# Normalization moved ahead, inner sums on POOL, chunk loads on SyncE and respread sums in a fused attention and feed-forward kernel

## The chip, the cores and the metric

The kernel runs on one core of one Trainium2 chip. The metric is the device time of one execution in microseconds, the median of several runs. The engines of the core are TensorE (PE in the profile, its weight loads PEld), VectorE (DVE), ScalarE (ACT), GpSimd (POOL) and SyncE (SP), which here only issues transfers. Each engine runs its own instructions in order, and semaphores tie the engines together.

## What is computed

An attention with a hash mask, whose output becomes the tokens of a feed-forward layer with a sigmoid-approximated gelu:

```python
# q, k, v: (4, 8, 768, 64); proj: (64, 6); w_in: (512, 2048); w_out: (2048, 512)
q_bucket = np.sum((np.einsum('bhsd,dk->bhsk', q, proj) > 0) * 2 ** np.arange(6), axis=-1)
k_bucket = np.sum((np.einsum('bhsd,dk->bhsk', k, proj) > 0) * 2 ** np.arange(6), axis=-1)
mask = q_bucket[:, :, :, None] == k_bucket[:, :, None, :]
scores = np.where(mask, np.matmul(q, k.transpose(0, 1, 3, 2)) / np.sqrt(64), -1e9)
attn = np.exp(scores - np.max(scores, axis=-1, keepdims=True))
attn = attn / (np.sum(attn, axis=-1, keepdims=True) + 1e-09)
x = np.matmul(attn, v).transpose(0, 2, 1, 3).reshape(3072, 512)
h = x @ w_in
out = (h * (1.0 / (1.0 + np.exp(-1.702 * h)))) @ w_out
```

The weights arrive as 64-bit floats, and the kernel turns them into 32-bit ones itself.

## The kernel before

The program has three stages, and TensorE, VectorE, ScalarE and POOL run exactly in the order in which the program is written (`manual_schedule` for these four). SyncE's queue is not among them: the framework's planner orders the transfers on it by the times at which it expects them to be ready.

**Attention** (to about 316 us) works on 16 pairs of heads. `invert` and `norm` divide a pair's result by its sums, on VectorE; for the last pair they are written at the end of `attention`, after `next(ff)`, which emits the first step of the feed-forward layer. Meanwhile VectorE converts chunks of w_in (`convert`, six steps on VectorE and a square on ScalarE for each chunk of 512 columns, with a single buffer `raw` for the load). Two late chunks of w_in and the 16 chunks of w_out are converted during the next stage (`conversions`), and their loads are issued by ScalarE (`queue=nc.scalar`), each right after the fourth step of the chunk before has freed `raw`.

**The first product, x @ w_in** (about 316 to 612 us), is Strassen's scheme in Winograd's form with seven products instead of eight. The operands' sums are made ahead: `in_sums` (POOL, lines 211 to 214) for the weights, two column blocks a call, and `x_sums` (VectorE, lines 219 to 222, by `sums_b`) for the tokens; `x_sums` has four parts, of which the first gives t1, the second changes b12 in place, the third gives t2 and the fourth t4. Product 5 uses t1, product 7 the changed b12, product 6 uses t2 and product 4 uses t4. There are three groups of 1024 tokens and eight column blocks in each, 24 steps. Steps 0, 1 and 20 to 23 are written by `hidden`, a step each; steps 2 to 19 are nine pairs t = 1 to 9, written by `pair_of_steps`. In a pair, products 2 and 3 of both steps are themselves split once more (`nested`) into seven small products of 256 columns; the operands' inner sums are `nest_w` (POOL) for the weights and `nest_x` (lines 797 to 800, VectorE) for the activations, once for each group of tokens. After each small product VectorE adds it to a result (line 750), and the next small product that shares its PSUM bank waits for that addition. `u`, `v`, `c22` and `c21` are a step's results, copied or activated by ScalarE; `g_outer` forms four outer sums `t`, `v` from them on POOL, and `keep` stores each to `g_dram` by SyncE.

A pair has ten numbered places (`hook(1)` to `hook(10)`) at which other work is written between the products: steps of a conversion, `in_sums` for later blocks, `nest_w`, and, at a change of tokens (the end of t = 3 and 7, then t = 4 and 8), `x_sums` and `nest_x` for the next group. The order around the front half of a pair is `p1(0)`, hook 1, `p1(1)`, hook 2, `p6(0)`, hook 3, `p6(1)`, hook 4, `p5(0)`, hook 5, `p7(0)`; `old()` between them writes the small products that the pair before has left over, one at a time. Product 6 of the first step is `p6(0)`.

**The second product** (about 612 us to the end) runs seven of these outer products for each of three groups, 21 steps of seven products (`product_of_halves`, line 1080). `g_sums` (VectorE) forms the operands' sums one step ahead, `inner_sums` (POOL) those of w_out; in steps 5 and 6 a tiny copy into `mark` holds POOL until a result of the step before is there. In the last but one step, `after` writes the third part of `g_sums`, t2, twice.

Of the kernel before, what the change touches and what calls it, by code (L numbers as in the profile page):

```python
# [8 lines left out]
F32 = mybir.dt.float32  # L9
# [4 lines left out]
Alu = mybir.AluOpType  # L14
# [5 lines left out]
P = 128  # L20
# [18 lines left out]
def kernel(  # L39
# [17 lines left out]
    nc = tc.nc  # L57
# [82 lines left out]
    t_x = const.tile([P, 3, KC // 2, 512], F32, name="t_x")  # L140
# [67 lines left out]
    def sums_a(eng, a11, a12, s3, a22, s1, s2, s4, a21=None):  # L208

        a21 = s3 if a21 is None else a21  # L210
        return [lambda: eng.tensor_tensor(s1, a21, a22, op=Alu.add),
                lambda: eng.tensor_tensor(s3, a11, a21, op=Alu.subtract),
                lambda: eng.tensor_tensor(s2, s1, a11, op=Alu.subtract),
                lambda: eng.tensor_tensor(s4, a12, s2, op=Alu.subtract)]
# [12 lines left out]
    def quarters_in(cols):  # L227
        w = [w_in_sb[:, K2 * k : K2 * (k + 1), F2 * i + cols.start : F2 * i + cols.stop]
             for i in range(2) for k in range(2)]
        return w + [s_in[:, i, :, cols] for i in range(3)]  # L230
# [2 lines left out]
        x = [xT[:, K2 * k : K2 * (k + 1), (2 * sb + j) * XT : (2 * sb + j + 1) * XT] for k in range(2) for j in range(2)]  # L233
        return x + [t_x[:, i] for i in range(3)]

    def in_sums(t):
        return sums_a(nc.gpsimd, *quarters_in(slice(2 * t * P, (2 * t + 2) * P)))


    def load(ld, n, v_bufs=2):  # L240
# [42 lines left out]
    def attention(ff):  # L283
# [4 lines left out]
        with actx:  # L288
            ld = actx.enter_context(tc.tile_pool(name="ld", bufs=1))
            wk = actx.enter_context(tc.tile_pool(name="wk", bufs=2))  # L290
            cv = actx.enter_context(tc.tile_pool(name="cv", bufs=1))
# [212 lines left out]
            def norm(n):  # L504
                x, rs = x_of(n), accs.pop(n)
                nc.vector.tensor_tensor(x, x, rs.rearrange("p (t s) -> p t s", t=T), op=Alu.mult)
# [14 lines left out]
            x_sums = sums_b(nc.vector, *quarters_x(0))  # L521
# [88 lines left out]
            for f in in_sums(0):  # L610
                f()
            early.close()
            next(ff)
            whole(invert(last))
            norm(last)


    def shifted_attention():
# [76 lines left out]
    def feed_forward(tag, late=()):  # L695
# [9 lines left out]
        with ExitStack() as fctx:  # L705
# [84 lines left out]
            def nest_x(sb, rooms):  # L790
                sums = {}
                for o in TWICE:
                    b = quarters_x(sb)[RIGHT[o]]
                    b11, b12, b21, b22 = (b[:, k, j * TH : (j + 1) * TH] for k in range(2) for j in range(2))
                    t1, d12, t2, t4 = ([rooms.pop(0)] + [rooms.pop(0) for _ in range(3)])
                    X[o, sb] = [b11, d12, b21, b22, t1, t2, t4]
                    sums[o] = [lambda a=t1, b=b12, c=b11: nc.vector.tensor_tensor(a, b, c, op=Alu.subtract),
                               lambda a=t2, b=b22, c=t1: nc.vector.tensor_tensor(a, b, c, op=Alu.subtract),
                               lambda a=d12, b=b22, c=b12: nc.vector.tensor_tensor(a, b, c, op=Alu.subtract),
                               lambda a=t4, b=b21, c=t2: nc.vector.tensor_tensor(a, b, c, op=Alu.subtract)]  # L800
                return sums

            def nested(o, sb, t, base, done):
# [313 lines left out]
            def conversions(cv, psum, chunks):  # L1117


                gens = [convert(cv, *x, queue=nc.scalar, psum=psum) for x in chunks]  # L1120
                next(gens[0])
                yield
                for i, x in enumerate(gens):
                    for at in range(6):
                        next(x, None)
                        if at == 3 and i + 1 < len(gens):
                            next(gens[i + 1])
                        yield

            def on(i, *fs):  # L1130
                hooks[i] = hooks.get(i, []) + list(fs)

            hidden(0, 0, in_sums(1))
            yield
            twice = twice_ctx.enter_context(tc.tile_pool(name=f"tw{tag}", bufs=1, side="right"))
            wop = fctx.enter_context(tc.tile_pool(name=f"wo{tag}", bufs=1))
# [30 lines left out]
            places = [[x[:, j * TH : (j + 1) * TH] for x in y for j in range(2)] for y in places]  # L1167
            more = nest_x(0, places[0])
            x = todo.pop(1, [])
            hidden(0, 1, nest_w(1) + more[2] + x[:4], x[4:] + more[3])  # L1170
            yield
            small_ctx.close()
            inner_ctx = fctx.enter_context(ExitStack())
# [2 lines left out]
            for t in NESTED:  # L1176
                sb, at = divmod(t, MT // 2)
                hooks = {}
                if at == 0:
                    on(1, x_sums[3], more[2][0])  # L1180
                    for i, f in zip((2, 4, 5, 6, 7, 8, 9), more[2][1:] + more[3]):
                        on(i, f)
                for n, places_of in ((2 * t, (1, 2, 2, 3, 3, 4)), (2 * t + 1, (6, 7, 7, 7, 9, 9))):
                    x = todo.pop(n, [])
                    for i in places_of:
                        on(i, *x[:1])
                        x = x[1:]
                    on(5 if n % 2 == 0 else 10, *x)
                if t + 1 < MT // 2:
                    on(5, *in_sums(t + 1))  # L1190
                    on(8, *nest_w(t + 1))
                elif t + 1 == MT // 2:
                    on(5, *nest_w(0))
                if at == MT // 2 - 1:
                    x_sums = sums_b(nc.vector, *quarters_x(sb + 1))
                    more = nest_x(sb + 1, places[sb + 1])
                    for i in range(3):
                        on(8 + i, x_sums[i])
                whole(pair_of_steps(t, hooks))
                yield  # L1200
            turn[0] = -1
# [20 lines left out]
            for n, (sb, o) in enumerate(steps_out):  # L1222
                final = n + 1 == len(steps_out)
                if 0 < n and n + 1 < len(steps_out):
                    fetch(n + 1)

                if n in (5, 6):
                    nc.gpsimd.tensor_copy(mark, ms[OUTER[n - 1]][0:1, 0, 0:1])
                for f in {0: inner_sums(4), 5: inner_sums(5) + inner_sums(6)[:2], 6: inner_sums(6)[2:]}.get(n, []):
                    f()  # L1230
                later_sums = g_sums(n + 1)
                m = wholes[n % len(wholes)]

                def after(at):
                    if at == 0:
                        while pending:
                            pending.pop(0)()

                    steps = [later_sums[at : at + 1]] if n == 0 else [[], later_sums[0:1], later_sums[1:3], later_sums[3:], []][at : at + 1]

                    if n + 2 >= len(steps_out):
                        turns = [lambda q=q: turned(m, int(final), int(not final), q, q + 1) for q in range(4)]
                        if final:
                            steps = [[[], [], [turns[1], turns[3]], [turns[2]], [turns[0]]][at]]
                        elif at == 3:
                            steps = [later_sums[2:3], turns[0:2], turns[3:4], later_sums[3:], turns[2:3]]
                    for f in sum(steps, []):
                        f()
                    if final and at in (2, 3):
                        written(sb, 0, (3 - at,), loader + [nc.scalar])  # L1250
                    if n + 2 == len(steps_out) and at == 3:
                        written(sb, 1, (0, 1), loader + [nc.scalar])

                acc = {6: 1, 7: 6, 2: 1, 3: 6, 4: 7}.get(o)
                if o == 3:
                    pending.pop(0)()
                ms[o] = product_of_halves(n, None if acc is None else ms[acc], after)
# [67 lines left out]
```

## Time and profile before

| what | us |
|---|---|
| median of 3 runs (877.57 to 879.08) | 878.31 |
| the profiled execution | 879.71 |
| its span on the core | 877.0 |
| TensorE matmuls, busy in it | 855.3 |
| VectorE busy | 711.8 |
| ScalarE busy | 339.5 |
| POOL busy | 328.9 |

Times in rows of the timeline are microseconds from the start of the span: start, duration, engine, line, operation, output <- input, partitions x elements, count, and in brackets the idle time of the engine just before with what ended it. A window's row holds its bounds and length, then for each engine the busy time with the number of instructions, then the granted clock of TensorE, the busy share of the DMA engines and GB/s; where only one line's records are asked for, the engines without any are left out. Matmuls overlap, so the distance from start to start is the pace, not the duration of a record. A float32 matmul appears as two records.

### The profile page before, as it was taken

To read this page: it belongs to the slowest core of one execution; us is meant where nothing else is said; L and a number is where in the kernel's file an instruction comes from. 1 tells how busy PE (TensorE), PEld (TensorE's weight loads), DVE (VectorE), ACT (ScalarE), POOL (GpSimd) and SP (SyncE) were. 2 spreads that over 40 slices of the span, in tenths; PEclk is the share of its full clock that TensorE was granted. 3 is DMA by queue.
4 is the path that set the end of the run, shared out by engine and by line. 5 is a ranking of instruction groups with operands and counts; after the bars stand their busy time and mean duration, and the time that the engine had idled before them with its cause. 6 is when DMAs were issued, how large, how long until landed. Compare 5 with 4: busy or idle time off the path is not lost.

```text
span 877.0 us, 13681 instructions
## 1 busy us (share of the span) xinstructions
PE 855.3 (98%) x4953; PEld 518.9 (59%) x4953; DVE 711.8 (81%) x1057; ACT 339.5 (39%) x567; POOL 328.9 (38%) x291
## 2 busy tenths in 40 slices
PE   9999999999999998899999999999999999999995
PEld 4444444444444443455555554544888888888884
DVE  4589999999999886776977788656797977897786
ACT  5766677776667632333343333343000000000000
POOL 4242233342234385547633444779913100000000
PEclk9999999999999999999999999999999999999998
DMA  6636645555642104435555556558744675467524
GB/s 132 95 60 106 98 83 84 88 122 95 101 86 82 36 1 170 150 109 194 197 187 204 203 193 207 201 186 319 250 177 171 198 246 197 166 203 240 192 96 99
DMA packets 169163, 132.12 MB, mean 151 GB/s; under 512 B 123616, under 2 KB 138112, under 8 KB 163712
## 3 DMA queue, kind: packets, MB, share of 16 engines
q1 hardware_dynamic: 163936, 120.26, 48.2%
q10 hardware_dynamic: 5152, 10.90, 4.5%
q8 instruction: 41, 0.67, 0.3%
q14 instruction: 34, 0.28, 0.1%
HBM read 79.69 MB, written 50.33 MB: 148 GB/s over the span
## 4 chain that ended last, share of the span: by engine, by line
PE 87%; DVE 8%; issue 1%; ACT 1%; POOL 1%; DMA 1%; ACTq 0%; SPq 0%; DVEq 0%; POOLq 0%
PE product L1080 26%; PE product L740 22%; PE ps L432 17%; PE av L465 14%; PE small L814 5%; DVE xT L1084 1%; PE dn L486 1%; PE hash L408 1%; DVE v L750 1%; DMA q<-in_q_dram 1%; ACT e L433 1%; DVE y L1060 1%; DVE u L750 0%; DVE acc L448 0%; DVE t2a L221 0%
## 5 line engine op out<-in xcount | busy, mean ns | idle before, releaser
L433 ACT ACTIVATE e<-ps 128x768 f32<-128x768 f32 x192 | 151.2, 812 | 25.8 <-PE ps L432 23.2
L432 PE MATMUL ps<-qT,kT 64*128 64x384 f32 x768 | 155.1, 482 | 0.0
L465 PE MATMUL av<-e,v 128*32 128x385 f32 x1536 | 128.0, 487 | 0.0
L440 POOL TENSOR_TENSOR acc<-e 128x768 f32<-128x768 f32 x32 | 51.8, 1618 | 193.7 <-ACT e L433 174.2
L740 PE MATMUL product<-xT,w_in_sb 128*128 128x512 f32 x216 | 103.7, 610 | 3.5 <-ACT v L967 2.6
L465 PEld LDWEIGHTS av<-e,v 128*32 128x32 f32 x1536 | 48.5, 109 | 76.3 <-issue 74.6
L432 PEld LDWEIGHTS ps<-qT,kT 64*128 64x128 f32 x768 | 68.0, 187 | 38.5 <-issue 38.4
L740 PE MATMUL product<-t_x,s_in 128*128 128x512 f32 x192 | 89.3, 592 | 0.2 <-ACT u L947 0.2
L219 POOL TENSOR_TENSOR t<-v,u 128x512 f32<-128x512 f32 x24 | 34.5, 1436 | 112.0 <-ACT v L747 112.0
L1093 ACT COPY u<-product 128x256 f32<-128x256 f32 x21 | 7.8, 372 | 174.5 <-PE product L1080 141.3
L740 PEld LDWEIGHTS product<-xT,w_in_sb 128*128 128x128 f32 x216 | 41.9, 196 | 41.6 <-issue 33.7
L432 PE MATMUL ps<-qf,kf 64*128 64x384 bf16 x384 | 62.9, 324 | 0.1
L441 POOL TENSOR_TENSOR acc<-acc,e 128x768 f32<-128x768 f32 x32 | 55.8, 1744 | 2.5
L740 PEld LDWEIGHTS product<-t_x,s_in 128*128 128x128 f32 x192 | 36.4, 190 | 31.5 <-issue 28.2
L446 DVE SCALAR_TENSOR_TENSOR acc<-e 128x768 f32<-128x768 f32 x32 | 47.7, 1490 | 5.1 <-ACT e L433 5.1
L740 PE MATMUL product<-t_x,w_in_sb 128*128 128x512 f32 x96 | 45.3, 594 | 0.0
L750 DVE TENSOR_TENSOR v<-small,v 128x256 f32<-128x256 f32 x63 | 26.0, 418 | 22.6 <-PE small L814 22.3
L432 PEld LDWEIGHTS <-kf 64*128 64x128 bf16 x384 | 18.9, 94 | 35.1 <-DMA q<-in_q_dram 6.2
L448 DVE TENSOR_TENSOR acc<-acc,e 128x768 f32<-128x768 f32 x32 | 34.3, 1072 | 3.3
L448 DVE TENSOR_TENSOR acc<-acc,acc 128x768 f32<-128x768 f32 x32 | 31.7, 991 | 6.3 <-POOL acc L441 3.2
L222 POOL TENSOR_TENSOR t<-c,t 128x512 f32<-128x512 f32 x24 | 35.2, 1468 | 1.9
L1080 PE MATMUL product<-raw_g,xT 128*128 128x256 f32 x152 | 35.1, 379 | 0.0
(241 smaller groups left out, 1644.7 us busy)
## 6 DMA issues: line engine op xcount, KB each, us to landing
raw_g<-g_dram SPq DMA_DIRECT2D x22, 1024.0 KB
s_in<-g_dram SPq DMA_DIRECT2D x20, 1024.0 KB
g_dram<-t SPq DMA_DIRECT2D x72, 256.0 KB
g_dram<-c SPq DMA_DIRECT2D x48, 256.0 KB
raw<-in_moe_w_out_dram ACTq DMA_DIRECT2D x16, 512.0 KB
raw<-in_moe_w_in_dram SPq DMA_DIRECT2D x14, 512.0 KB
v<-in_v_dram SPq DMA_DIRECT2D x32, 192.0 KB
g_dram<-u SPq DMA_DIRECT2D x24, 256.0 KB
```

The costliest lines, as they stand in the source:

```text
L222: lambda: eng.tensor_tensor(t4, b21, t2, op=Alu.subtract)]
L432: nc.tensor.matmul(ps[:, j, 0:HS], a[hs, keys], m[hs, cols], start=not last, stop=last)
L433: nc.scalar.activation(es[c][:, kt, :, 0:HS], ps[:, :, 0:HS], Act.Exp, scale=1.0 / D**0.5)
L440: nc.gpsimd.tensor_tensor(acc, es[c][:, 0, :, 0:HS], es[c][:, 1, :, 0:HS], op=Alu.add)
L441: nc.gpsimd.tensor_tensor(acc, acc, es[c][:, 2, :, 0:HS], op=Alu.add)
L446: nc.vector.scalar_tensor_tensor(acc, e[0], T * TINY, e[1], op0=Alu.add, op1=Alu.add)
L448: nc.vector.tensor_tensor(acc, acc, x, op=Alu.add)
L465: nc.tensor.matmul(av[D * j + d : D * j + d + 32, :], vt[:, t, j, d : d + 32], es[c][:, t, j, :], start=(t == 0), stop=(t == T - 1))
L740: nc.tensor.matmul(ps, wq[LEFT[i]][:, kc, :], xq[RIGHT[i]][:, kc, :], start=(start and kc == 0), stop=(kc == K2 - 1), skip_group_check=not ...
L750: nc.vector.tensor_tensor(dst, x, y, op=Alu.add)
L814: nc.tensor.matmul(ps[at], wq[LEFT[i]], xq[RIGHT[i]], start=start, stop=True, skip_group_check=not start)
L1080: nc.tensor.matmul(ps, wq[LEFT[i]][:, c, :], gq[RIGHT[i]][:, c, :], start=(c == 0), stop=(c == F4 - 1))
```

## The change

The change has five parts.

1. At the end of `attention`, `invert(last)` and `norm(last)` come before `next(ff)`. `in_sums(0)` now covers one column block instead of two. At the head of the feed-forward layer POOL copies one element of the last x sum into `behind_sums` and then forms the sums of blocks 1 to 3, where before it formed those of 2 and 3 in the middle of step 0. Later calls cover the same blocks as before.
2. `nest_x`, eight operations for each of three groups, runs on POOL.
3. The loads of the 18 chunks go to SyncE's queue. In step 1, the inner sums of both kinds stand ahead of the conversion steps.
4. At a change of tokens only the first of the x sums stays in the pair before (hook 10); the others stand at hooks 1, 2 and 4 of the new pair, the inner sums in twos at hooks 1 to 4, and the conversion steps from hook 3 on.
5. In the output stage, `inner_sums(4)` moves from step 0 to steps 2 and 3, each half behind a `mark`; the second t2 of the last but one step is dropped.

```diff
-    def in_sums(t):
-        return sums_a(nc.gpsimd, *quarters_in(slice(2 * t * P, (2 * t + 2) * P)))
+    def in_sums(mt, count=1):
+        return sums_a(nc.gpsimd, *quarters_in(slice(mt * P, (mt + count) * P)))
...
             early.close()
-            next(ff)
             whole(invert(last))
             norm(last)
+            next(ff)
...
-                    sums[o] = [lambda a=t1, b=b12, c=b11: nc.vector.tensor_tensor(a, b, c, op=Alu.subtract),
+                    sums[o] = [lambda a=t1, b=b12, c=b11: nc.gpsimd.tensor_tensor(a, b, c, op=Alu.subtract),
...
-                gens = [convert(cv, *x, queue=nc.scalar, psum=psum) for x in chunks]
+                gens = [convert(cv, *x, psum=psum) for x in chunks]
...
-            hidden(0, 0, in_sums(1))
+            behind_sums = stage.tile([1, 1], F32, name="behind_sums", bufs=1)
+            nc.gpsimd.tensor_copy(behind_sums, t_x[0:1, 2, 0, 0:1])
+            for f in in_sums(1) + in_sums(2, 2):
+                f()
+            hidden(0, 0)
...
-            hidden(0, 1, nest_w(1) + more[2] + x[:4], x[4:] + more[3])
+            hidden(0, 1, more[2] + nest_w(1) + more[3] + x[:4], x[4:])
...
                 if at == 0:
-                    on(1, x_sums[3], more[2][0])
-                    for i, f in zip((2, 4, 5, 6, 7, 8, 9), more[2][1:] + more[3]):
+                    for i, fs in zip((1, 2, 3, 4), (more[2][:2], more[2][2:], more[3][:2], more[3][2:])):
+                        on(i, *fs)
+                    for i, f in zip((1, 2, 4), x_sums[1:]):
                         on(i, f)
-                for n, places_of in ((2 * t, (1, 2, 2, 3, 3, 4)), (2 * t + 1, (6, 7, 7, 7, 9, 9))):
+                    places_of = (3, 4, 4, 5, 6, 6), (7, 8, 9, 9, 10, 10)
+                else:
+                    places_of = (1, 2, 2, 3, 3, 4), (6, 7, 7, 7, 9, 9)
+                for n, late_by in zip((2 * t, 2 * t + 1), places_of):
...
                 if t + 1 < MT // 2:
-                    on(5, *in_sums(t + 1))
+                    on(5, *in_sums(2 * t + 2, 2))
...
-                    for i in range(3):
-                        on(8 + i, x_sums[i])
+                    on(10, x_sums[0])
...
-                if n in (5, 6):
+                if n in (2, 3, 5, 6):
                     nc.gpsimd.tensor_copy(mark, ms[OUTER[n - 1]][0:1, 0, 0:1])
-                for f in {0: inner_sums(4), 5: inner_sums(5) + inner_sums(6)[:2], 6: inner_sums(6)[2:]}.get(n, []):
+                for f in {2: inner_sums(4)[:2], 3: inner_sums(4)[2:], 5: inner_sums(5) + inner_sums(6)[:2], 6: inner_sums(6)[2:]}.get(n, []):
...
                         elif at == 3:
-                            steps = [later_sums[2:3], turns[0:2], turns[3:4], later_sums[3:], turns[2:3]]
+                            steps = [turns[0:2], turns[3:4], later_sums[3:], turns[2:3]]
```

More of the change, by code (lines that the diff above doesn't have):

```diff
@@ L796, in nest_x @@
                     X[o, sb] = [b11, d12, b21, b22, t1, t2, t4]
-                    sums[o] = [lambda a=t1, b=b12, c=b11: nc.vector.tensor_tensor(a, b, c, op=Alu.subtract),
-                               lambda a=t2, b=b22, c=t1: nc.vector.tensor_tensor(a, b, c, op=Alu.subtract),
-                               lambda a=d12, b=b22, c=b12: nc.vector.tensor_tensor(a, b, c, op=Alu.subtract),
-                               lambda a=t4, b=b21, c=t2: nc.vector.tensor_tensor(a, b, c, op=Alu.subtract)]
+                    sums[o] = [lambda a=t1, b=b12, c=b11: nc.gpsimd.tensor_tensor(a, b, c, op=Alu.subtract),
+                               lambda a=t2, b=b22, c=t1: nc.gpsimd.tensor_tensor(a, b, c, op=Alu.subtract),
+                               lambda a=d12, b=b22, c=b12: nc.gpsimd.tensor_tensor(a, b, c, op=Alu.subtract),
+                               lambda a=t4, b=b21, c=t2: nc.gpsimd.tensor_tensor(a, b, c, op=Alu.subtract)]
                 return sums
@@ L1179, in feed_forward @@
                 if at == 0:
-                    on(1, x_sums[3], more[2][0])
-                    for i, f in zip((2, 4, 5, 6, 7, 8, 9), more[2][1:] + more[3]):
+                    for i, fs in zip((1, 2, 3, 4), (more[2][:2], more[2][2:], more[3][:2], more[3][2:])):
+                        on(i, *fs)
+                    for i, f in zip((1, 2, 4), x_sums[1:]):
                         on(i, f)
-                for n, places_of in ((2 * t, (1, 2, 2, 3, 3, 4)), (2 * t + 1, (6, 7, 7, 7, 9, 9))):
+                    places_of = (3, 4, 4, 5, 6, 6), (7, 8, 9, 9, 10, 10)
+                else:
+                    places_of = (1, 2, 2, 3, 3, 4), (6, 7, 7, 7, 9, 9)
+                for n, late_by in zip((2 * t, 2 * t + 1), places_of):
                     x = todo.pop(n, [])
-                    for i in places_of:
+                    for i in late_by:
                         on(i, *x[:1])
```

## The prediction

> **What bounds the kernel now.** I read the page first, then the chain of waits, TensorE's records in windows, and the timeline around every hole.
>
> ```profile
> span 877.0 us, 13681 instructions
> PE 87%; DVE 8%; issue 1%; ACT 1%; POOL 1%; DMA 1%; ACTq 0%; SPq 0%; DVEq 0%; POOLq 0%
> 572.10 39.81 PE product L740 x92
> 642.63 209.18 PE product L1080 x968
> ```
>
> The chain that ended last is 87% TensorE, so TensorE sets the end; the change removes no matmul and can only win TensorE's holes. The two chain rows give the undisturbed pace: 39.81/92 = 0.433 us for a 512-column record and 209.18/968 = 0.216 us for a 256-column one. The windows hold records against time, first L740's and then the small products of L814:
>
> ```profile
> 315.88:345.08 29.20, 26.46 (x56) 11.14 (x57) 0.94 0.28 100
> 345.08:371.20 26.12, 19.91 (x41) 8.11 (x40) 0.93 0.40 137
> 345.08:371.20 26.12, 4.58 (x16) 3.11 (x16) 0.93 0.40 137
> 420.21 1.88 PE L740 MATMUL product<-xT,w_in_sb 128*128 128x512 f32 x4
> 445.49 1.88 PE L740 MATMUL product<-xT,w_in_sb 128*128 128x512 f32 x4
> 491.91 1.88 PE L740 MATMUL product<-xT,w_in_sb 128*128 128x512 f32 x4
> 515.12 1.88 PE L740 MATMUL product<-xT,w_in_sb 128*128 128x512 f32 x4
> 540.14 1.88 PE L740 MATMUL product<-xT,w_in_sb 128*128 128x512 f32 x4
> ```
>
> Steps 0 and 1 (first window): 56 x 0.433 = 24.2 of 29.2 us, so **5.0 us** lost. Pair t=1 (second): 40 x 0.433 + 16 x 0.216 = 20.8 of 26.1, **5.3 us** lost. A clean pair lasts 515.12 - 491.91 = 23.2 us from one `p1(1)` to the next; the pair after the first change of tokens (t=4) lasts 25.3 and after the second (t=8) 25.0, **3.9 us** lost together. The output stage has two holes:
>
> ```profile
> 642.63 1.97 PE L1080 MATMUL product<-t2a,w_in_sb 128*128 128x256 f32 x8 [1.36 <-DVE t2a L221]
> 859.43 1.99 PE L1080 MATMUL product<-t2a,s_in 128*128 128x256 f32 x8 [0.73 <-DVE t2a L221]
> ```
>
> That is 2.1 us more. About 16 us is all there is to win.
>
> **The change part by part.**
>
> *Steps 0 and 1.*
>
> ```profile
> L178 DVE SCALAR_TENSOR_TENSOR w_in_sb<-raw,mask_3fffffff x14: 681/684/1772, 67.3 to 314.3; 128x512 uint32<-128x512 uint32 x14
> 324.41 2.29 DVE L222 TENSOR_TENSOR t_x<-xT,t_x 128x1024 f32<-128x1024 f32 x1
> 331.16 0.57 DVE L492 STREAM_TRANSPOSE rt<-dn 128x384 f32<-128x384 f32 x1
> 334.07 1.33 DVE L506 TENSOR_TENSOR xT<-xT,rs 128x768 f32<-128x768 f32 x1
> 335.48 0.34 ACTq L162 DMA_DIRECT2D raw<-in_moe_w_in_dram  x1
> 335.86 0.58 ACT L967 COPY v<-product 128x512 f32<-128x512 f32 x1 [3.96 <-DVE xT L506]
> 336.50 5.32 PE L740 MATMUL product<-xT,w_in_sb 128*128 128x512 f32 x8 [2.55 <-ACT v L967]
> 336.50:340.20 3.70, 3.70 (x5) 1.70 (x6) 0.00 (x0) 0.06 (x1) 3.43 (x7) 0.56 0.79 277
> ```
>
> ScalarE's in-order queue holds the load of the first late chunk, whose space frees only after `norm(last)` (L506). TensorE's next product needs the copy behind that load: 2.55 us of hole, and then 3.7 us at a granted clock of 0.56, about 1.7 us more. The change moves the norm ahead and the load to SyncE, so both causes go. The moved norm now stands before the additions. It costs little there. One conversion step takes 0.68 us and took 1.77 in the last chunk, from 314.3 on, beside POOL's sums; with half of these cut off and held behind L222 by `behind_sums`, six steps of 0.7 us and some first contention end near 319.3, and L222 (1.2 us alone) near 320.5 instead of 326.7. Inversion and norm (331.16 to 335.40, 4.2 us) then end near 325. Products are 1.73 us each from 315.9: the first addition needs the fifth (324.6) and ScalarE's copy (0.6), so it is due near 325.3. The sums for step 1, 3 us of POOL from 320.6, are needed by the ninth product at 329.7. I take the full 5.0 us; bounds 2.5 (the hole alone) to 5.0.
>
> *Pair t=1.*
>
> ```profile
> 346.87 0.33 ACTq L162 DMA_DIRECT2D raw<-in_moe_w_in_dram  x1
> 347.90 1.98 PE L740 MATMUL product<-xT,w_in_sb 128*128 128x512 f32 x4 [0.93 <-ACT c L747]
> 350.79 0.65 ACT L190 ACTIVATE size<-raw 128x512 f32<-128x512 f32 x1 [0.29 <-DMA raw<-in_moe_w_in_dram]
> 352.74 1.48 DVE L800 TENSOR_TENSOR w_out_sb<-xT,w_out_sb 128x256 f32<-128x256 f32 x1
> 354.14 0.68 DVE L180 TENSOR_SCALAR part<-raw 128x512 uint32<-128x512 uint32 x1
> 359.55 0.67 PE L814 MATMUL small<-w_out_sb,w 128*128 128x256 f32 x2 [2.37 <-issue]
> ```
>
> Two holes: ScalarE again behind a load (0.93), then 2.37 us (and a slow clock behind it) because the small product needs an addition that queues behind six conversion steps from 354.14, themselves behind four inner sums ending with L800 at 354.22. Moved to POOL, those four sums leave VectorE. A late chunk now decides: a load takes 350.79 - 346.87 = 3.9 us. If SyncE issues the first load once the norm has freed its space, near 325, nothing is late and 5.3 us come back. If it stands behind the four stores of step 0's outer sums, it lands about 0.8 us after pair 1 begins; VectorE's addition to `v`, ScalarE's gelu and the copy of `u` follow it, and TensorE waits some 1.9 us at `p6(0)`. I take 5.0, nearer the first, because the order on SyncE's queue is not the program's (below); bounds 1.8 to 5.3.
>
> *The moved inner sums.*
>
> ```profile
> L211 POOL TENSOR_TENSOR w<-w_in_sb 128x128 f32<-128x128 f32 x4 | 1.8, 454 | 0.0
> 431.89 1.27 POOL L219 TENSOR_TENSOR t<-v,u 128x512 f32<-128x512 f32 x1 [6.82 <-ACT v L747]
> ```
>
> The 24 operations of 128x256 lie between these rows of POOL, 0.45 and 1.27 us: about 0.73 us, an estimate in proportion to the columns. In step 1 POOL has four outer sums, eight of these and eight weight sums: 4 x 1.27 + 8 x 0.73 + 8 x 0.45 = 14.5 us from 331.5, when step 0's `v` is written, to 346. Pair 1 begins near 340 (345.1 less 5.0), and its first small product that uses an inner sum comes after six products and a small one, 10.8 us later: covered by 5 us, at 1.27 us each by 0.5. Without that cover they would cost what they overrun.
>
> *The changes of tokens* are where I expect a **loss**.
>
> ```profile
> 414.27 1.61 DVE L219 TENSOR_TENSOR t_x<-xT 128x1024 f32<-128x1024 f32 x1
> 421.93 0.59 PE L814 MATMUL small<-w_out_sb,w 128*128 128x256 f32 x2
> 422.36 1.88 PE L740 MATMUL product<-t_x,s_in 128*128 128x512 f32 x4
> 539.17 0.70 PE L814 MATMUL small<-xT,w 128*128 128x256 f32 x2 [1.41 <-DVE v L750]
> ```
>
> Product 6 of the first step (422.36) multiplies by t2, which `x_sums[2]` writes. Before, that sum stood at hook 10 of the pair ahead and was ready. Now it stands at hook 2, directly ahead of `p6(0)`, and behind the addition of the small product at 421.93, whose result is there at 422.4. So VectorE can start it only near 422.8; at 1.2 us alone or 1.6 beside POOL (414.27) product 6 starts at 424.0 to 424.5: a new hole of 1.7 to 2.1 us, in bad phase 2.6. POOL's eight inner sums run right then. The spreading takes away the old stalls, but hook 4 now holds one x sum and two conversion steps ahead of an addition that the small product after `p7(0)` needs; I count 0.7 us. Half clock after the hole: 1.41 us (539.17) shows none, 2.37 and 2.55 do, so I give 2.1 an even chance below that, 0.4 us. 2.1 + 0.7 + 0.4 = 3.2 us twice against 3.9 before: **+2.5 us**. Bounds: -3.9 (every stall gone) to +6.2 (2.6 + 1.7 + 0.75 twice, less 3.9).
>
> VectorE's 128x256 inner sum took 1.48 us beside POOL (L800). The Trainium skill ("SBUF — State Buffer", Who interferes with whom) says that a VectorE instruction with two SBUF inputs and a GpSimd one that reads SBUF exclude each other for a whole instruction. By that rule, which that row bears out, moving sums to POOL beside x sums can hold `x_sums[2]` for one whole POOL operation, and the loss would be up to 0.9 us larger at each change (1.2 + 1.27 against 1.6). The skill's "TensorE: Matmul & The Clock Gate" (What's actually happening) puts the half clock after an idle window of about 3.4 us; by it the new holes would cost no clock and the sum would be 0.8 us better. Here it came after 2.55 us, so the measurement decides.
>
> *SyncE's queue.*
>
> ```profile
> 390.36 0.33 ACTq L162 DMA_DIRECT2D raw<-in_moe_w_out_dram  x1
> 391.50 0.63 ACT L747 ACTIVATE c<-c 128x512 f32<-128x512 f32 x1 [3.00 <-DVE c L750]
> 397.54 0.68 DVE L180 TENSOR_SCALAR part<-raw 128x512 uint32<-128x512 uint32 x1
> 403.53 0.89 SPq L744 DMA_DIRECT2D g_dram<-c  x2
> ```
>
> SyncE is in order but its order is the planner's, and that plan holds POOL for faster than it is: the c written by 392.13 is stored only at 403.53, behind stores of POOL's sums. A chunk load planned there is late too. In pair t=2 POOL also forms weight sums; a load that ScalarE issued at 390.36 goes out on SyncE somewhere up to 403.5; landing 3.9 us later, it is up to 9.8 us late for the conversion at 397.54. About 2.1 us of that is slack (one product and one small one), so TensorE loses 0 to 7.7 us. The load is ready a microsecond ahead of that c, so I take an early place, 0.7 us; the other pairs have no such backlog.
>
> *Output stage.* VectorE is late with t2 at 642.63 because `inner_sums(4)` ran beside its additions; spread over two steps, half of it still lies there and half later, and VectorE gains more than the 1.4 us it lacked: 1.4 won, bounds 0 to 1.4. In the last but one step the second, identical t2, which TensorE waits for at 859.43, is gone: some 1.2 us of VectorE, **0.9 us** at the end, since the hole goes and the last stores follow VectorE's transposes; bounds 0.7 to 1.2.
>
> Sum: 5.0 + 5.0 - 2.5 - 0.7 + 1.4 + 0.9 = **9.1 us**. The profiled execution took 879.71 us (span 877.0 and 2.7 around it), 1.4 above the median of the runs, so 870.6 for it and 878.31 - 9.1 = **869.2** for the median.
>
> **The rivals.**
>
> *The changes cost nothing*: VectorE runs ahead enough, or product 6 doesn't wait. For it: the mean addition is soon done; against it: the order above. 5.0 + 5.0 + 3.9 + 1.4 + 0.9 = 16.2 us, 862.1.
>
> *SyncE holds two loads*: the first chunk behind step 0's stores (1.6 us more) and the one in pair 2 halfway into POOL's sums (3.9 instead of 0.7): 874.0, at the very worst 877.8. For it: c waits that way; against it: both loads are ready ahead of what would hold them.
>
> *Slower: SyncE holds every second load of a pair until the pair's last store.*
>
> ```profile
> 468.89 2.02 SPq L744 DMA_DIRECT2D g_dram<-u  x1
> 469.25 0.68 DVE L180 TENSOR_SCALAR part<-raw 128x512 uint32<-128x512 uint32 x1
> ```
>
> Issued at 470.9 with 3.9 us to land, a load would be 5.5 us late for VectorE at 469.25; less the slack of 2.1, 3.4 us a time. Seven pairs: 23.8 less the 0.7 counted, 892.3. It decides from a lateness of 2.1 us on. For it: c waits that way in every pair; against it: the load is ready before the c that waits.
>
> *It does nothing*: the early holes move to another wait of the same length (pair 1 starts with a chunk still on its way) and the changes lose what the output wins; 876.6 to 880.
>
> **How the numbers follow.** Forecast 52% (own range 866 to 873), the changes cost nothing 18%, two loads held 13%, slower 8%, nothing 6%, forms between 3%. 861.5 to 876.5 leaves out the slower case, the empty one and some tails. Differences under 0.2% (1.8 us) can't be told from none; faster by more than that 85%, the same 7%, slower 8%.
>
> **What would show it.** Right: no load on ScalarE's queue; TensorE unbroken from 316 to pair 1 in about 24.3 us at full clock; pair 1 near 21 us; at t=4 and t=8 product 6 waiting about 2 us for VectorE's `t_x` (L221); one t2 in the last but one step. Wrong: TensorE waiting at small products while conversions wait for `raw`, stores of t ahead of a `raw` on SyncE, or no hole at product 6.

## The result and the profile after

| | before | after |
|---|---|---|
| median, us (range, runs) | 878.69 (877.57 to 882.94, 4) | 869.76 (868.91 to 870.54, 4) |
| the profiled execution, us | 879.71 | 868.91 |
| its span, us | 877.0 | 867.1 |

The ratio of the times is 0.9889, with a 95% interval of 0.9855 to 0.9924. The forecast was 869.2 us. Outside the span, the profiled execution took 2.7 us before and 1.8 after.

The page of the changed kernel, its span and the chain that ended last:

```profile
span 867.1 us, 13723 instructions
PE 91%; DVE 4%; POOL 2%; DMA 1%; issue 1%; SPq 0%; ACT 0%; ACTq 0%; DVEq 0%; POOLq 0%
```

TensorE sets the end more than before (91% of the chain, 87% before). Its windows, by the bounds that the forecast used: steps 0 and 1, pair t=1, an undisturbed pair (t=2) and the pairs after the changes of tokens (t=4 and t=8), the last three each from one `p1(1)` to the next:

```profile
316.39:340.53 24.14, 24.14 (x60) 10.75 (x57) 14.09 (x23) 10.81 (x18) 17.97 (x20) 1.00 0.34 120
340.53:361.69 21.16, 20.86 (x58) 10.56 (x57) 14.32 (x25) 7.35 (x13) 19.16 (x27) 1.00 0.44 142
364.79:388.00 23.21, 23.21 (x70) 12.92 (x68) 16.98 (x31) 9.35 (x16) 12.61 (x11) 1.00 0.29 104
411.23:437.87 26.64, 23.69 (x70) 12.76 (x69) 21.74 (x34) 9.46 (x16) 20.14 (x18) 1.00 0.61 211
507.49:532.97 25.48, 23.69 (x69) 12.75 (x68) 20.51 (x33) 9.47 (x16) 15.90 (x14) 1.00 0.51 174
```

Steps 0 and 1 fell from 29.20 to 24.14 us and pair 1 from 26.12 to 21.16, at full clock. The changes of tokens lost more than before: 26.64 - 23.21 = 3.43 and 25.48 - 23.21 = 2.27, together 5.7 against 3.9. The timeline of TensorE shows where, and the rows of VectorE and POOL at the first change, with VectorE's t2 at the second, show why:

```profile
416.04 1.96 PE L740 MATMUL product<-t_x,s_in 128*128 128x512 f32 x4 [2.50 <-DVE t_x L221]
425.32 0.67 PE L814 MATMUL small<-xT,w 128*128 128x256 f32 x2 [0.45 <-DVE u L750]
511.58 1.95 PE L740 MATMUL product<-t_x,s_in 128*128 128x512 f32 x4 [1.77 <-DVE t_x L221]
...
410.36 2.25 POOL L221 TENSOR_TENSOR t<-c,t 128x512 f32<-128x512 f32 x1
412.07 1.62 DVE L220 TENSOR_TENSOR xT<-xT 128x1024 f32<-128x1024 f32 x1
412.69 2.12 POOL L222 TENSOR_TENSOR t<-c,t 128x512 f32<-128x512 f32 x1
413.62 0.41 DVE L750 TENSOR_TENSOR v<-small,v 128x256 f32<-128x256 f32 x1
413.95 1.95 DVE L221 TENSOR_TENSOR t_x<-xT,t_x 128x1024 f32<-128x1024 f32 x1
...
510.18 1.25 DVE L221 TENSOR_TENSOR t_x<-xT,t_x 128x1024 f32<-128x1024 f32 x1
```

Product 6 waits for the third x sum, t2, which begins at 413.95, after the second sum and an addition, and takes 1.95 us beside POOL's sums. They lengthen each other: t2 took 1.25 us at the second change (last row), and POOL's outer sums took 2.25 and 2.12 us here against 1.27 in the forecast's row at 431.89. Product 6 was due at 416.04 - 2.50 = 413.54, and t2 began 0.41 us after that; at the second change it began 0.37 us after. The forecast had 0.44, so in these two holes only the length of t2 differs from it.

Two small waits are new, one at the end of pair 1 and one at the start of the next pair. SyncE's rows and VectorE's wait explain them:

```profile
325.19 0.34 SPq L162 DMA_DIRECT2D raw<-in_moe_w_in_dram  x1
340.80 0.33 SPq L162 DMA_DIRECT2D raw<-in_moe_w_in_dram  x1
350.45 1.66 SPq L744 DMA_DIRECT2D g_dram<-t  x2
352.28 0.33 SPq L162 DMA_DIRECT2D raw<-in_moe_w_out_dram  x1
...
356.01 0.69 DVE L180 TENSOR_SCALAR part<-raw 128x512 uint32<-128x512 uint32 x1 [2.57 <-DMA raw<-in_moe_w_out_dram]
360.75 0.67 PE L814 MATMUL small<-xT,w 128*128 128x256 f32 x2 [0.30 <-DVE u L750]
363.85 0.67 PE L814 MATMUL small<-w_out_sb,w 128*128 128x256 f32 x2 [0.29 <-DVE v L750]
```

The first load goes out at 325.19, right after the normalization. The third stands behind two stores of outer sums, lands 3.7 us after 352.28, and holds VectorE for 2.57 us; TensorE then waits 0.3 twice for VectorE's additions. In the output stage both waits for t2 are gone.

The start of the second product tells the sums apart: from the first product of the first stage to there, 611.75 - 315.89 = 295.86 us became 604.73 - 316.39 = 288.34; from there to the start of the last product, 254.70 became 252.09.

### The profile page after: what moved, and what is told of

It is laid out like the page before. It is cut to its first block, busy times and chain, and to the rows that moved or that the text cites. A ratio compares the mean times of both kernels' runs of the same rounds, so it can differ in the third digit from the quotient of the medians.

```text
span 867.1 us, 13723 instructions
## 1 busy us (share of the span) xinstructions
PE 850.9 (98%) x4953; PEld 517.9 (60%) x4953; DVE 686.4 (79%) x1032; ACT 340.4 (39%) x567; POOL 344.0 (40%) x322
## 4 chain that ended last, share of the span: by engine, by line
PE 91%; DVE 4%; POOL 2%; DMA 1%; issue 1%; SPq 0%; ACT 0%; ACTq 0%; DVEq 0%; POOLq 0%
PE product L1080 27%; PE product L740 22%; PE ps L432 18%; PE av L465 15%; PE small L814 6%; PE dn L486 1%; PE hash L408 1%; DVE xT L1084 1%; DMA q<-in_q_dram 1%; DVE v L750 1%; DVE y L1060 1%; DMA raw<-in_moe_w_out_dram 0%; DVE t_x L221 0%; POOL v L220 0%; POOL t L219 0%
## 5 line engine op out<-in xcount | busy, mean ns | idle before, releaser
L740 PE MATMUL product<-xT,w_in_sb 128*128 128x512 f32 x216 | 100.2, 593 | 0.0
L750 DVE TENSOR_TENSOR u<-small,u 128x256 f32<-128x256 f32 x63 | 25.5, 417 | 11.1 <-PE small L814 8.0
```

Source lines behind the costliest of these rows:

```text
L740: nc.tensor.matmul(ps, wq[LEFT[i]][:, kc, :], xq[RIGHT[i]][:, kc, :], start=(start and kc == 0), stop=(kc == K2 - 1), skip_group_check=not ...
L750: nc.vector.tensor_tensor(dst, x, y, op=Alu.add)
```

## The experiments

Eleven kernels ran. Unless a median is named, each has one profiled execution; the kernel before took 877.30 beside the first four, 878.42 (median) beside the next four, 878.36 beside the first two of the last three and 878.80 (median) beside the last.

**x sums ahead again** (part 4 undone in its main piece).

```diff
-                    for i, f in zip((1, 2, 4), x_sums[1:]):
-                        on(i, f)
+                    on(1, x_sums[3])
...
-                    on(10, x_sums[0])
+                    for i in range(3):
+                        on(8 + i, x_sums[i])
```

> The changed kernel with the first three x sums back at hooks 8, 9 and 10 of the pair ahead and the fourth at hook 1; the inner sums stay on POOL and the conversion steps stay late. Theory: the two holes at product 6 (2.50 and 1.77 us in the changed kernel) come from the place of the third x sum alone; both go, p1(1) to p1(1) falls from 26.6 to 23.2-24.0 us at t=4 and from 25.5 to 23.2-24.0 at t=8, and the span falls from 867.1 to 862.5-864. Rival: VectorE lacks the time wherever these sums stand, and the old stalls at the small products come back (3.9 us lost at the two changes before): 25.2 us each, span about 865.5. Second rival: POOL's sums in the same stretch hold VectorE and the time stays at 867.

863.38 us, span 861.6. The windows of the pairs at the two changes, and VectorE's t2:

```profile
411.18:434.39 23.21, 23.21 (x69) 12.92 (x68) 18.55 (x32) 9.55 (x16) 20.70 (x19) 1.00 0.68 244
504.02:527.23 23.21, 23.21 (x69) 12.92 (x68) 18.12 (x32) 9.55 (x16) 16.90 (x16) 1.00 0.61 215
...
410.02 1.63 DVE L221 TENSOR_TENSOR t_x<-xT,t_x 128x1024 f32<-128x1024 f32 x1
```

Nothing is lost at either change. t2 is done at 411.65, and product 6 starts at 413.33, though POOL's sums run beside it here too. The pair ahead of the first change, where the sums now stand, loses 0.3. So the place of the sums cost nearly the whole 5.7 us: from the first product of the first stage to the start of the second product takes 282.74 us here and 288.34 in the changed kernel.

**Only t1 and t2 ahead.**

```diff
-                    for i, f in zip((1, 2, 4), x_sums[1:]):
+                    for i, f in zip((1, 4), (x_sums[1], x_sums[3])):
...
-                    on(10, x_sums[0])
+                    on(8, x_sums[0])
+                    on(10, x_sums[2])
```

> The changed kernel with two x sums in the pair ahead, the first at hook 8 and the third (t2) at hook 10; the second stays at hook 1 and the fourth at hook 4 of the new pair. Theory: only t2 stood in the way, since it is what product 6 multiplies by; the holes go as they went with three sums ahead (26.6 and 25.5 us fell to 23.21 each), up to 0.5 us each for the fourth sum at hook 4, which stands ahead of an addition for a small product (0.45 in the changed kernel): span 861.6 to 862.6. Rival: it was the number of x sums in the front of the new pair, not t2's place: with two of them still there 1 to 2 us are lost at each change, span 864 to 866.

864.03 us, span 862.2; no wait at product 6, and one of 0.25 us at the addition behind the fourth sum:

```profile
422.25 0.67 PE L814 MATMUL small<-xT,w 128*128 128x256 f32 x2 [0.25 <-DVE u L750]
```

So t2 is the sum that must not stand in the new pair; the other two may, for 0.25 us.

**Loads on ScalarE's queue again**, in the changed kernel and then in the one with three x sums ahead.

```diff
-                gens = [convert(cv, *x, psum=psum) for x in chunks]
+                gens = [convert(cv, *x, queue=nc.scalar, psum=psum) for x in chunks]
```

> The changed kernel with the chunk loads on ScalarE's queue again; normalization first as in the change. Theory: what made ScalarE stand at 336 us was the late normalization, not its queue. With the norm ended near 325 the load finds its space free, steps 0 and 1 stay at 24.1 us (29.2 before), and the load of the third chunk, which SyncE issued at 352.28 behind two stores, comes earlier, so that the small waits in pair 1 (0.30 and 0.29) go: span 866 to 867. Rival: ScalarE's queue was the cause by itself: its copies wait behind a load again and TensorE shows a hole of 2 to 3 us in step 1 and one of about 0.9 at the start of pair 1: 870 to 873.

868.62 us, span 866.0. Steps 0 and 1 and pair 1:

```profile
316.50:340.64 24.14, 24.14 (x60) 10.75 (x57) 14.09 (x23) 10.30 (x17) 17.96 (x20) 1.00 0.34 120
340.64:361.26 20.62, 20.62 (x57) 10.64 (x56) 15.50 (x26) 8.75 (x15) 19.14 (x27) 1.00 0.54 173
```

No hole comes back, and pair 1 loses its small wait (20.62 against 21.16). So ScalarE's queue makes no hole once the normalization is early and the first weight sums are cut.

> The kernel with three x sums ahead (span 861.6) with the chunk loads on ScalarE's queue. Theory: SyncE's order costs the late third chunk and nothing else; the waits of about 0.3 and 0.28 us in pair 1 and the first pair behind it go: span 860.8 to 861.3, about 862.6 us. Rival: ScalarE's issues delay its copies at the changes, where x sums and inner sums leave no slack, and one or more holes of 0.3 to 1 us open: span 862 to 863.

Median of five 863.05 us (862.45 to 864.11), 0.9826 of the kernel before (95%: 0.9810 to 0.9843), span 859.6. TensorE has no listed wait left behind the attention. From its first product to the second stage it takes 597.27 - 315.48 = 281.79 us, against 598.97 - 316.23 = 282.74 with loads on SyncE: SyncE's order cost 0.95 us of this stage. (A kernel below that differs from the latter only in the output stage takes 283.10 there, so such a difference is known to about 0.4 us.) The span came out below what was expected, 0.75 us of it because the first product began earlier. The device time does not tell the two apart: 863.38 us in the one execution with loads on SyncE lies within 862.45 to 864.11, since 1.8 us lie outside the span there and 2.9 here. Why is not shown.

**The normalization behind the first step**, loads on SyncE.

```diff
+            next(ff)
             whole(invert(last))
             norm(last)
-            next(ff)
```

> The changed kernel with the first step of the feed-forward layer written ahead of the last normalization again; loads on SyncE as in the change. Theory: the two edits need each other. SyncE's order then has the first load behind all eight stores of step 0, the last of which went out at 337.4; it lands 3.9 us later, near 341.4, where VectorE wants it at 337.9. Steps 0 and 1 stay near 24.2 us, but VectorE's addition to v behind the conversion steps is some 4 us late, and TensorE waits 2 to 3 us at the first products of pair 1, with or without a slow clock behind it: span 869 to 872. Rival: the queue alone freed ScalarE and the place of the norm is worth nothing: 867.

871.57 us, span 869.8. The load on SyncE, VectorE's wait for it, and TensorE:

```profile
336.98 0.36 SPq L162 DMA_DIRECT2D raw<-in_moe_w_in_dram  x1
341.61 0.70 DVE L180 TENSOR_SCALAR part<-raw 128x512 uint32<-128x512 uint32 x1 [4.88 <-DMA raw<-in_moe_w_in_dram]
342.80 1.98 PE L740 MATMUL product<-xT,w_in_sb 128*128 128x512 f32 x4 [1.64 <-ACT c L747]
346.36 5.39 PE L740 MATMUL product<-t_x,s_in 128*128 128x512 f32 x12 [1.58 <-ACT u L851]
```

As expected, steps 0 and 1 last 24.14 us (315.13 to 339.27) and the loss stands in pair 1: two waits, 3.2 us. (The span also holds a half clock at the first change, told last.) With the late normalization and loads on SyncE the loss stands in pair 1 instead of step 1; the early normalization takes it away. No run has the late normalization with the loads on ScalarE beside the cut weight sums, so what the queue gives by itself is not shown.

**No hold on POOL's sums.**

```diff
-            nc.gpsimd.tensor_copy(behind_sums, t_x[0:1, 2, 0, 0:1])
+            nc.gpsimd.memset(behind_sums, 0.0)
```

> The changed kernel in which the tiny copy behind the last x sum is a memset that waits for nothing, so that POOL's sums for the column blocks 1 to 3 can start as soon as their weights are there. Theory: the hold is what keeps VectorE's conversion steps (1.22, 1.11 and 1.11 us, then 0.69) and its last x sum (1.22) short; without it they stretch towards the 1.77 and 2.29 us of before, the normalization ends 2 to 4 us after 325.0, the first addition (325.9) is late by as much, and steps 0 and 1 grow from 24.1 to 25-27 us. Rival: POOL is held by the converted weights anyway, or the delay has slack: 24.1 us and span 867 as with the hold.

869.54 us, span 867.7. VectorE is late, as expected, but TensorE isn't: steps 0 and 1 last from 315.84 to 339.98, 24.14 us again.

```profile
326.74 0.68 DVE L750 TENSOR_TENSOR c<-product,c 128x512 f32<-128x512 f32 x1
```

In time from the first product that addition starts 10.9 us in, 1.4 later than with the hold (325.90 - 316.39 = 9.5), and nothing waits for it. The rival holds. (The span is 0.6 us longer because of a half clock at the first change, told last; its 1.7 us are in part made up by a first product 0.55 us earlier and by the wait of 0.45 us behind the first change, which isn't there.)

**Inner sums of the activations on VectorE**, in the kernel with three x sums ahead.

```diff
-                    sums[o] = [lambda a=t1, b=b12, c=b11: nc.gpsimd.tensor_tensor(a, b, c, op=Alu.subtract),
+                    sums[o] = [lambda a=t1, b=b12, c=b11: nc.vector.tensor_tensor(a, b, c, op=Alu.subtract),
...
```

> The kernel with three x sums ahead (span 861.6) with the 24 inner sums of the activations on VectorE again. Theory: POOL's taking them is what pair 1 and the changes live on. In step 1 eight sums of 0.6 to 1.5 us then stand ahead of the conversion steps and of the addition to v (340.7), which comes some 4 us late: 2.5 to 4 us lost at the head of pair 1 (20.98 us now), and 0.5 to 2 us at each change (23.21 now): span 865 to 869. Rival: with the norm ahead and the conversions late VectorE has room for them (8 x 0.6 us in each stretch): 861.6 to 862.5, and the move to POOL is worth nothing.

868.60 us, span 865.6.

```profile
344.95 0.68 DVE L750 TENSOR_TENSOR v<-product,v 128x512 f32<-128x512 f32 x1
346.91 5.39 PE L740 MATMUL product<-t_x,s_in 128*128 128x512 f32 x12 [2.77 <-ACT u L851]
425.89 0.67 PE L814 MATMUL small<-xT,w 128*128 128x256 f32 x2 [0.92 <-DVE u L750]
```

The addition to `v` comes at 344.95 instead of 340.57 (VectorE's row in the kernel with three x sums ahead) and TensorE waits 2.77 us. At the first change TensorE waits 0.92 us and the pair loses 24.49 - 23.21 = 1.28; at the second it loses nothing. The move to POOL is worth 4.0 us of span. The changes lose 1.3 us here and 3.9 in the kernel before, with the x sums at the same places: spreading the inner sums and conversion steps takes away two thirds of the old stalls even with the inner sums on VectorE.

**The output stage as before**, in the kernel with three x sums ahead (both diffs of part 5 reversed).

> The kernel with three x sums ahead (span 861.6) with the output stage as before: inner sums of product 5's weights in step 0, and t2 written twice in the last but one step. Theory: the hole of 1.36 us at the t2 of the second step returns, and 0.7 to 1.2 us at the end (0.73 at the last step's product and the stores behind it): span 863.5 to 864.2. Rival: with the stages ahead shortened the two have slack, or the end is set by the stores: 861.6 to 862.3.

865.94 us, span 864.1.

```profile
629.84 1.97 PE L1080 MATMUL product<-t2a,w_in_sb 128*128 128x256 f32 x8 [1.37 <-DVE t2a L221]
846.64 1.99 PE L1080 MATMUL product<-t2a,s_in 128*128 128x256 f32 x8 [0.73 <-DVE t2a L221]
```

Both waits of before return; the stage up to its last product takes 254.70 us instead of 252.09, as before. Part 5 is worth 2.5 us of span.

**Built up from the kernel before.** First the swap of `next(ff)` and the normalization alone, then with `nest_x` on POOL and part 5.

> The kernel before with one edit: the last normalization ahead of the first step's additions. Theory: this alone removes the hole at 336.5 and the slow clock behind it (steps 0 and 1: 29.20 to 24.1-24.4 us), with the loads still on ScalarE's queue and nothing held; pair 1 still has VectorE's inner sums ahead of the conversion steps, so 1 to 4 of its 5 lost us stay; the changes of tokens and the output stage lose what they lost before: span 868.5 to 871. Rival: the gain needs the other parts too (the load's queue or POOL's sums cut in half): VectorE is late with the first additions and steps 0 and 1 keep 2 us or more of their 5: span 873 to 876.

> The kernel before with three edits: the normalization ahead, the 24 inner sums of the activations on POOL, and the output stage's two edits; loads on ScalarE, no hold, x sums and conversion steps at their old places. Theory: these three carry the whole gain, and the other parts add nothing or cost: 877.0 less 5.0, 5.3, 2.6 and up to 3.9 at the changes, span 859.6 to 861.5, as with x sums ahead and loads on ScalarE (859.6). Rival: the conversion steps at the front of the changes still hold additions there, and 0.5 to 2 us stay at each: span 862 to 864.

876.62 us, span 874.6, and 867.78, span 865.4. Of the first the theory failed and the rival, that the gain needs other parts too, held; of the second both failed. In both TensorE waits 2.50 us in step 0, in the first

```profile
331.49 1.96 PE L740 MATMUL product<-xT,s_in 128*128 128x512 f32 x4 [2.50 <-DVE c L750]
331.49:333.28 1.79, 1.79 (x4) 0.84 (x5) 0.45 (x1) 1.60 (x3) 0.00 (x0) 1.00 0.23 81
316.08:343.58 27.50, 24.82 (x60) 10.50 (x57) 19.95 (x25) 10.12 (x17) 17.76 (x17) 1.00 0.30 106
343.58:368.68 25.10, 21.13 (x57) 10.47 (x56) 22.81 (x33) 8.49 (x15) 14.55 (x18) 1.00 0.42 143
```

and in the second

```profile
323.32 1.57 DVE L198 SCALAR_TENSOR_TENSOR w_in_sb<-raw,w_in_sb 128x512 f32<-128x512 f32 x1
330.00 0.96 DVE L506 TENSOR_TENSOR xT<-xT,rs 128x768 f32<-128x768 f32 x1
331.70 3.31 PE L740 MATMUL product<-xT,s_in 128*128 128x512 f32 x4 [2.50 <-DVE c L750]
331.70:335.20 3.50, 3.50 (x5) 1.62 (x6) 0.60 (x2) 1.61 (x3) 0.00 (x0) 0.57 0.54 197
316.30:345.49 29.19, 26.51 (x60) 11.09 (x57) 19.88 (x24) 10.13 (x17) 18.02 (x19) 0.94 0.28 100
345.49:366.11 20.62, 20.62 (x57) 10.64 (x56) 15.52 (x26) 8.76 (x15) 19.00 (x24) 1.00 0.51 172
```

The conversion steps still take 1.57 to 1.77 us beside POOL's sums of two column blocks, the normalization ends at 330.96 instead of 325.04, and the additions are late. Steps 0 and 1 last 27.50 us in the first kernel, at full clock, and 29.19 in the second, with half clock behind the hole: as long as the 29.20 of before. So the early normalization without the cut sums trades one hole for another. Pair 1 falls from 25.10 to 20.62 us between the two, which is what the inner sums on POOL do there. And at the changes, with x sums and conversion steps at their old places, the second of these kernels loses nothing (23.21 us for each pair). What was missing is the cut of the first weight sums:

```diff
-    def in_sums(t):
-        return sums_a(nc.gpsimd, *quarters_in(slice(2 * t * P, (2 * t + 2) * P)))
+    def in_sums(mt, count=1):
+        return sums_a(nc.gpsimd, *quarters_in(slice(mt * P, (mt + count) * P)))
...
-            hidden(0, 0, in_sums(1))
+            hidden(0, 0, in_sums(1) + in_sums(2, 2))
...
-                    on(5, *in_sums(t + 1))
+                    on(5, *in_sums(2 * t + 2, 2))
```

> The kernel before with four edits: the three of the last run (normalization ahead, inner sums of the activations on POOL, the output stage's two) and the first weight sums cut from two column blocks to one, as in the change; loads on ScalarE, no hold, x sums and conversion steps at their old places. Theory: the cut is what the three edits lacked. VectorE's six conversion steps shrink from 1.57-1.77 us each to 1.0-1.2, the normalization ends near 326 instead of 330.96, the hole of 2.50 us before product 2 of step 0 and the slow clock behind it go, and nothing else is lost: span 859.5 to 860.5, about 863 us, as the changed kernel with x sums ahead and loads on ScalarE (863.05). Rival: the sums held behind the last x sum and the late conversion steps count after all: 1 to 3 us lost in step 0 or at the changes, span 861 to 864.

Median of five 862.26 us (861.94 to 863.04), 0.9811 of the kernel before (95%: 0.9797 to 0.9824); span 860.9.

```profile
320.57 1.03 DVE L198 SCALAR_TENSOR_TENSOR w_in_sb<-raw,w_in_sb 128x512 f32<-128x512 f32 x1
326.16 1.62 DVE L506 TENSOR_TENSOR xT<-xT,rs 128x768 f32<-128x768 f32 x1
316.80:340.94 24.14, 24.14 (x61) 10.75 (x57) 16.23 (x23) 10.24 (x17) 20.00 (x21) 1.00 0.34 120
340.94:361.55 20.61, 20.61 (x57) 10.64 (x56) 15.47 (x26) 8.74 (x15) 19.30 (x25) 1.00 0.53 172
410.56:433.77 23.21, 23.21 (x70) 12.92 (x68) 18.53 (x33) 9.42 (x16) 19.69 (x19) 1.00 0.68 233
```

The cut makes the difference of 4.5 us in span between the last two kernels; about 1.7 of it is the half clock, which the first of the three built-up kernels didn't have at the same hole. The normalization ends at 327.78, later than expected and later than in the changed kernel (325.04), and nothing waits for it. This kernel beats both kernels of the study, without part 3, without the hold, and without part 4.

## Why the forecast held, point by point

| term | forecast, us | measured, us |
|---|---|---|
| steps 0 and 1 | +5.0 | +5.06 |
| pair t=1 | +5.0 | +4.96 |
| changes of tokens | -2.5 | -1.8 |
| SyncE's order elsewhere | -0.7 | -0.5 behind pair 1 (0.95 in all) |
| up to the start of the last product in the output | +2.3 with the tail | +2.6 |
| the tail behind it | in the row above | +0.3 |
| first product later than before | not foreseen | -0.5 |

The measured terms sum to 10.1 us; the span fell by 9.9, and the other 0.2 are small stalls later in the first product. The last two rows are no larger than what differs between executions: the changed kernel and the six variants of it that alter nothing in the attention and keep the normalization early and the hold have their first product between 315.48 and 316.50, and the tail lasted 10.55 us before, 10.28 after and 10.2 to 10.5 in these variants.

That the median came within 0.6 us of the forecast is in part luck. The changes lost 0.7 us less and the output won 0.6 more than forecast, the first product began 0.5 later, and no half clock fell on either change in the profiled execution, while the kernel without the hold had one at the same place. The profiled execution was forecast at 870.6 and took 868.91; 0.9 us of that lie outside the span, which the forecast took as equal.

*Steps 0 and 1.* Size right, cause half right. The forecast gave the hole to ScalarE's queue and the late normalization together and said that both go. The runs show that the queue is no cause once the normalization is early and the sums are cut (24.14 us with loads on ScalarE), and that with the normalization late and loads on SyncE the loss stands in pair 1 (3.2 us of waits). It named the cut and the hold in one breath for VectorE's conversion steps; the cut is needed (without it a wait of 2.50 us stands at another product and up to the whole 5 us is lost again), and the hold buys 1.4 us of VectorE that nobody waits for. The cut without the early normalization was not run.

*Pair 1.* Right. VectorE's inner sums were the large hole: moving them to POOL takes pair 1 from 25.10 to 20.62 us in the kernels built up from before, and back on VectorE they cost a wait of 2.77 us there, at another product. The early of the two places for the first load came true (325.19). The forecast's mechanism for the other case was right too, in the third load.

*The changes.* Right in kind: product 6 waits for t2 at both. The term was mis-sized from both ends. The forecast put the hole at 1.7 to 2.1 and counted 2.1; it was 2.50 and 1.77. With 0.7 us at hook 4 (0.45 at the first change, no such wait listed at the second) and 0.4 of slow clock (none in that execution), 6.4 us were expected and 5.7 came. The 2.50 is what it priced as the bad phase (2.6). The Trainium skill ("SBUF — State Buffer", Who interferes with whom) allowed up to 0.9 us more there, and the trace agrees: t2 took 1.95 us at the first change, where POOL's sum at 412.69 was still running when it began, against 1.25 at the second. One sentence of this step gave half the cause: that the spreading takes the old stalls away. POOL's inner sums do that without it (0 us lost with sums and conversion steps at their old places); the spreading without them leaves 1.3 of 3.9.

*SyncE.* The cost came by the foreseen way, a load behind stores of POOL's sums, but in pair 1 and not in pair 2.

*Output.* Both holes went as forecast; the stage up to its last product won 2.6 us.

The rival by which the changes cost nothing gave 862.1 us. That is what the kernels give that keep the x sums where they were and load through ScalarE: 862.26 and 863.05. The slower rival, SyncE holding every second load, didn't come: VectorE waited 8.8 us in six waits for chunks of w_out, the longest 3.09 us (for the conversion at 391.72), and behind all of them TensorE shows only the two waits of 0.3 us.

## What to carry to other kernels

When a queue stands behind a late event, look at moving the event before the queue. Here the early event was worth 5 us in steps 0 and 1, but only together with the cut of the sums that slowed the engine ahead of it; the other queue cost about 1 us of the stage and nothing that the device time shows. A sum that feeds the first product of a new group belongs ahead of the group's first products, however crowded the engine is there; what frees that engine is to hand other sums to one with time to spare. And a change of many parts wants each part tried from both ends, since taking the hold away showed nothing of the cut beside it.

## What the hardware showed that was not expected

A hole in TensorE's work is followed by half clock or by none, and its length doesn't decide it. Two windows, of the changed kernel and of the one without the hold, right behind the wait for t2 at the first change:

```profile
416.04:417.83 1.79, 1.79 (x4) 0.84 (x5) 0.00 (x0) 0.00 (x0) 1.71 (x3) 1.00 1.02 377
```

```profile
415.28:418.80 3.52, 3.52 (x5) 1.60 (x6) 0.00 (x0) 0.09 (x1) 3.36 (x6) 0.55 0.69 259
```

The hole was 2.50 us ahead of the first and 2.41 ahead of the second. The two kernels built up from before show it at one place with one length: 2.50 us, then a granted clock of 1.00 in one and 0.57 in the other. Over all runs, behind the attention, holes of 2.37, 2.41, 2.44, 2.50 and 2.55 us were followed by some 3.5 us of half clock, holes of 2.37, 2.50, 2.50 and 2.77 us by none, and those of 1.87 us and less by none. So a hole of 2.4 to 2.8 us costs its length and, in five of these nine cases, about 1.7 us more (steps 0 and 1 of the two built-up kernels: 27.50 and 29.19 us); the forecast gave it an even chance. The Trainium skill ("TensorE: Matmul & The Clock Gate", What's actually happening) says that the clock is halved after an idle window of about 3.4 us, and that this window runs free. The holes here are shorter than that, and five of them were followed by half clock all the same; the measurement decides. That the same hole goes both ways fits a window that runs free; no run shows the window itself.
